# Top-k attention and a gated feed-forward: from pairs of heads to tiles of queries, with the mask on ScalarE and the gate on GpSimd

## The chip, the cores and the metric

The kernel runs on one core of one Trainium2 chip. The metric is the device time of one execution in microseconds (us). The engines are named as in the profile: PE is TensorE's matmuls and PEld its weight loads, DVE is VectorE, ACT is ScalarE, POOL is GpSimd, SP is SyncE, which here only issues DMAs.

## What is computed

Eight batches of eight heads attend over 576 tokens of 64 dimensions. Of every row of scores only the 32 largest (and what equals the 32nd) are kept. The result, 4608 tokens of 512, goes through two matrix products with a gate between them. The weights arrive in float64.

```python
def attention(q, k, v):                       # (8, 8, 576, 64) each, float32
    scores = np.matmul(q, k.transpose(0, 1, 3, 2)) / np.sqrt(64)
    kth = np.partition(scores, -32, axis=-1)[..., -32:-31]
    scores = np.where(scores >= kth, scores, -1e9)
    attn = np.exp(scores - scores.max(axis=-1, keepdims=True))
    attn = attn / (attn.sum(axis=-1, keepdims=True) + 1e-9)
    return np.matmul(attn, v)

def feed_forward(x, w_in, w_out):             # (4608, 512), (512, 2048), (2048, 512)
    h = x @ w_in
    return (h * np.cos(h)) @ w_out
```

## The kernel before

Attention goes by units: 128 queries of two heads (a pair), or the 64 left-over queries of both heads together in one tile. There are 160 units, 128 whole ones and 32 of 64 queries, so that DVE's work is that of 144 whole ones. They run batch by batch, and within a batch pair by pair; the five units of a pair follow one another.

`scores` (L111) lets PE write two tiles of 128 by 576 scores and ACT copy them to SBUF with the scale (L127). `softmax` finds the 32 largest on DVE: four rounds of MAX8 (L141), which gives the eight largest of a row, and three of MATCH_REPLACE (L153), which takes them out of a copy. After the first round POOL negates the maximum (L144) and ACT takes the exponential of all 576 (L146). After the fourth, DVE compares the scores with the 32nd, multiplies by the exponential and sums the row in one SCALAR_TENSOR_TENSOR (L156); then come the reciprocal on DVE (L167) and the normalising on POOL (L169). `transpose_p` (L191, L202) and `values` (L222) follow one unit behind, P times V only after two or three units, with 256 or 320 queries at once.

The feed-forward works on blocks of 384 tokens, three for every two batches. `ff1` (L250) makes two d_ff tiles of 384 tokens, ACT copies them out (L257), and POOL reduces the argument of the cosine in five instructions (L261 to L265). After every four items `gate` runs Abs (L270) and Sin (L272) on ACT and multiplies on DVE (L274). `ff2` (L280) needs a block's 16 tiles and makes 128 tokens by 512.

What sets the order is the loop at the end: scores one unit ahead, softmax, then as much of the feed-forward as a credit of streamed rows allows. A scheduler then gives each engine one fixed sequence, which the engine carries out in order. Weights are decoded from float64 in 16 pieces of 1024 columns, one per unit, by five DVE instructions, one of ACT and one of POOL each.

## Time and profile before

| | |
|---|---|
| three runs | 2244.55, 2256.88, 2257.63 us (median 2256.88) |
| profiled execution: span from first to last instruction | 2246.1 us (its own time is not listed apart) |
| PE / PEld / DVE / ACT / POOL busy | 1904.3 / 1020.7 / 1868.2 / 1059.5 / 985.9 us |
| mean granted TensorE clock | 0.887 of 2.4 GHz |
| DMA | 56.00 MB, mean 25 GB/s |

The profiled execution lies inside the spread of the runs, so its rows can be summed against the span; the median is 10.8 us above it. A float32 product of TensorE stands in the trace as two records, a transpose as one. Busy time counts overlapping instructions of an engine once, and a "mean ns of one" contains pipeline latency, so that rates are read from dense stretches.

### The profile page before, as it was taken

Reading aid. Unit: us, or ns where it says so; the run is one execution under the profiler, and the core shown is the slowest. Engines: PE = TensorE matmul, PEld = TensorE weight load, DVE = VectorE, ACT = ScalarE, POOL = GpSimd, SP = SyncE. Lnnn points to the kernel's source line nnn. Section 1 sums busy time; section 2 is a strip of 40 time slices with the busy share of each in tenths; the row PEclk is TensorE's granted clock in tenths of the full one; section 3 lists DMA queues with packets and bytes.
Section 4 is the critical chain, followed back from the end, with each engine's and each line's share of the span. In section 5 each row is a group of like instructions: output and inputs, shape, how many; then the busy total and the mean of one; then the engine's idle time right before and its main releaser. Section 6 shows DMA issues by size and latency. Waiting matters only on the chain.

```text
span 2246.1 us, 22954 instructions
## 1 busy us (share of the span) xinstructions
PE 1904.3 (85%) x7200; PEld 1020.7 (45%) x7200; DVE 1868.2 (83%) x3953; ACT 1059.5 (47%) x1706; POOL 985.9 (44%) x1078
## 2 busy tenths in 40 slices
PE   4556688978898898898899898898898898898878
PEld 2222244445644444446544444446544444447443
DVE  8999987998999979889998798998999799793000
ACT  3333355445545545645645635635645545643121
POOL 3444256114625524524725525615616515616362
PEclk9555688977999899899999899998898898999999
DMA  4222000000000000000000000000000000000000
GB/s 136 81 86 72 16 16 6 26 23 15 11 30 17 16 26 21 14 27 12 14 28 16 17 26 21 16 31 6 16 30 16 12 26 21 6 15 1 10 5 14
DMA packets 37305, 56.00 MB, mean 25 GB/s; under 512 B 2880, under 2 KB 21312, under 8 KB 36160
## 3 DMA queue, kind: packets, MB, share of 16 engines
q1 hardware_dynamic: 37184, 54.54, 7.4%
q8 instruction: 57, 0.93, 0.2%
q14 instruction: 64, 0.52, 0.1%
HBM read 45.09 MB, written 9.44 MB: 24 GB/s over the span
## 4 chain that ended last, share of the span: by engine, by line
DVE 36%; PE 22%; POOL 22%; ACT 10%; issue 10%; DMA 0%; POOLq 0%; SPq 0%; DVEq 0%; ACTq 0%
DVE m L141 14%; DVE rest L153 12%; PE o L280 8%; POOL r L264 6%; POOL r L265 5%; DVE pt L156 4%; PE sc L120 4%; POOL r L262 3%; POOL n L263 3%; PE o L222 3%; POOL n L261 3%; PE tp L191 2%; POOL pt L169 2%; ACT r L270 2%; ACT ht L257 2%
## 5 line engine op out<-in xcount | busy, mean ns | idle before, releaser
L141 DVE MAX8 m<-rest 128x8 f32<-128x576 f32 x864 | 616.2, 748 | 64.2 <-POOL neg L144 61.5
L280 PE MATMUL o<-w_out,ht 128*128 128x512 f32 x1152 | 539.3, 611 | 7.3 <-DVE ht L274 6.2
L120 PE MATMUL sc<-k,q 64*128 64x512 f32 (+3 forms) x1280 | 391.2, 518 | 164.9 <-ACT s L127 159.8
L153 DVE MATCH_REPLACE8 rest<-m,rest 128x576 f32<-128x576 f32 x576 | 423.7, 742 | 0.0
L120 PEld LDWEIGHTS sc<-k,q 64*128 64x128 f32 (+1 forms) x1280 | 165.7, 203 | 383.6 <-ACT s L127 215.9
L144 POOL TENSOR_SCALAR neg<-m 128x1 f32<-128x1 f32 x288 | 71.0, 251 | 599.0 <-DVE den L165 430.1
L169 POOL TENSOR_SCALAR pt<-pt,rden 128x576 f32<-128x576 f32 x288 | 253.2, 888 | 169.1 <-DVE rden L167 165.7
L280 PEld LDWEIGHTS o<-w_out,ht 128*128 128x128 f32 x1152 | 211.3, 194 | 233.0 <-issue 209.7
L156 DVE SCALAR_TENSOR_TENSOR pt<-s,m,pt 128x576 f32<-128x576 f32 x288 | 271.1, 974 | 53.0 <-ACT pt L146 52.7
L191 PE MATMUL tp<-ident,pt 128*128 128x128 f32 x1152 | 205.2, 322 | 116.8 <-POOL pt L169 114.6
L274 DVE TENSOR_TENSOR ht<-ht,r 128x768 f32<-128x768 f32 x96 | 100.1, 1054 | 214.2 <-ACT r L272 214.2
L146 ACT ACTIVATE pt<-s,neg 128x576 f32<-128x576 f32 x288 | 214.9, 772 | 113.0 <-POOL neg L144 112.1
L127 ACT ACTIVATE s<-sc 128x576 f32<-128x576 f32 (+1 forms) x320 | 201.5, 646 | 136.9 <-DVE pt L156 112.4
L191 PEld LDWEIGHTS tp<-ident,pt 128*128 128x128 f32 x1152 | 151.6, 162 | 230.7 <-POOL pt L169 195.6
L261 POOL TENSOR_SCALAR n<-ht 128x768 f32<-128x768 f32 x96 | 85.3, 888 | 378.5 <-ACT ht L257 375.2
L193 ACT COPY pT<-tp 128x512 f32<-128x512 f32 x256 | 141.3, 584 | 181.1 <-PE tp L191 179.0
L141 DVE MAX8 m<-s 128x8 f32<-128x576 f32 x288 | 214.2, 753 | 0.0
L153 DVE MATCH_REPLACE8 rest<-m,s 128x576 f32<-128x576 f32 x288 | 212.2, 742 | 0.0
L270 ACT ACTIVATE r<-r 128x768 f32<-128x768 f32 x96 | 81.0, 844 | 252.1 <-POOL r L265 252.1
L264 POOL TENSOR_TENSOR r<-r,ht 128x768 f32<-128x768 f32 x96 | 182.1, 1897 | 5.4
L265 POOL TENSOR_TENSOR r<-r,n 128x768 f32<-128x768 f32 x96 | 178.8, 1862 | 6.6
L222 PE MATMUL o<-pT,v 128*64 128x320 f32 (+1 forms) x1024 | 164.3, 471 | 0.9 <-ACT pT L196 0.5
(611 smaller groups left out, 2137.7 us busy)
## 6 DMA issues: line engine op xcount, KB each, us to landing
q<-in_q_dram SPq DMA_DIRECT2D x32, 288.0 KB, 2.9
k<-in_k_dram SPq DMA_DIRECT2D x32, 288.0 KB, 3.2
out_dram<-ob SPq DMA_DIRECT2D x36, 256.0 KB, 2.0
v<-in_v_dram SPq DMA_DIRECT2D x32, 256.0 KB, 2.8
st<-in_moe_w_in_dram SPq DMA_DIRECT2D x8, 1024.0 KB, 5.2
st<-in_moe_w_out_dram SPq DMA_DIRECT2D x8, 1024.0 KB, 4.9
v_tail<-in_v_dram SPq DMA_DIRECT2D x32, 32.0 KB, 2.4
```

The costliest lines, as they stand in the source:

```text
L120: nc.tensor.matmul(sc[j][rows[j], ks], st["q"][d, qs], st["k"][d, ks], start=True, stop=True)
L127: nc.scalar.mul(out=s[j % len(s)][rows[j]], in_=sc[j][rows[j]], mul=SCALE)
L141: nc.vector.max(m8[j], tops[j])
L146: nc.scalar.activation(out=pt[:, j], in_=s[j], func=AF.Exp, bias=neg[:, j : j + 1], scale=1.0)
L153: nc.vector.match_replace(rest[j], m8[j], tops[j], NEG)
L156: nc.vector.scalar_tensor_tensor(out=pt[:, j], in0=s[j], scalar=m8[j][:, 7:8], in1=pt[:, j], op0=ALU.is_ge, op1=ALU.mult, accum_out=den[:, ...
L169: nc.gpsimd.tensor_scalar(out=pt[:, j], in0=pt[:, j], scalar1=rden[:, j : j + 1], scalar2=1.0, op0=ALU.mult, op1=ALU.mult,)
L191: nc.tensor.transpose(tp[:, c], pt[:, j, c * P : (c + 1) * P], ident)
L222: nc.tensor.matmul(o[j * D : (j + 1) * D, 0:w], lhsT, rhs, start=c == 0, stop=c == NT)
L264: gp.tensor_tensor(out=r, in0=r, in1=ht, op=ALU.add)
L265: gp.tensor_tensor(out=r, in0=r, in1=n, op=ALU.add)
L280: nc.tensor.matmul(o[:, 0:DM], g[grp, blk, f // FI][:, f % FI, i * P : (i + 1) * P], w_out[:, f], start=f == 0, stop=f == NF - 1,)
```

## The change

The order of attention is now by tiles of queries: for one tile of 128 (or 64) queries all four pairs of heads follow one another, and P times V is done for each unit with its 128 (64) queries. Blocks of the feed-forward are 128 tokens (the first two and the last two) or 256 tokens, and are ready as soon as a tile, or two, of all heads are. The scores are taken two units ahead, in one PSUM tile with one copy of 1152 elements; `softmax`, transposes and P times V come one and two units later.

The mask leaves DVE. POOL makes two small numbers of the largest and the 32nd (`bounds`), ACT runs Prelu in place, whose slope for negative arguments is 2^100, and then Exp, which also sums the row. What is below the 32nd becomes so negative that its exponential is 0. DVE keeps MAX8, MATCH_REPLACE and the reciprocal.

In the feed-forward ACT already divides by 2 pi at the copy (L355), POOL reduces by four instructions of 1024 elements (L360 to L363), ACT runs Sin alone, and POOL multiplies (L379). The two products are cut into items: 512 columns of `ff1`, four d_ff tiles of `ff2`. `feed` picks one when its inputs are there, at two places of a unit. Weights are decoded in 32 pieces of 512 columns, four per unit, with three instructions each on ACT and DVE and two on POOL.

```diff
--- before.py
+++ after.py
...
-    BLK = 3 * P  # tokens in a block of the feed-forward
...
-    loads = ctx.enter_context(tc.tile_pool(name="loads", bufs=2))
+    loads = ctx.enter_context(tc.tile_pool(name="loads", bufs=5))
...
-    CW = 1024  # weights of a partition in a chunk
+    CW = 512
...
+        r = stage.tile([P, CW], I32, tag="lo", name="lo")
+        nc.scalar.mul(out=r, in_=lo.bitcast(U32), mul=2.0**-29)
+        sg = stage.tile([P, CW], F32, tag="sg", name="sg")
+        nc.scalar.sign(sg, hi)
+        nc.scalar.activation(out=w, in_=hi.bitcast(F32), func=AF.Abs)
+        nc.vector.tensor_scalar(out=w, in0=w, scalar1=2.0**-15, scalar2=None, op0=ALU.max)
+        nc.vector.tensor_scalar(
+            out=wi, in0=wi, scalar1=896 << 20, scalar2=3,
+            op0=ALU.bitwise_xor, op1=ALU.logical_shift_left,
+        )
+        nc.vector.tensor_scalar(
+            out=wi, in0=wi, scalar1=0x7FFFFFFF, scalar2=None, op0=ALU.bitwise_and
+        )
+        nc.gpsimd.tensor_tensor(out=wi, in0=wi, in1=r, op=ALU.add)
+        nc.gpsimd.tensor_tensor(out=w, in0=w, in1=sg, op=ALU.mult)
+    units = []
+    for b in range(B):
+        if b % 2 == 0:
+            tiles = [(i * P, P) for i in range(NT)] + [(MAIN, TAIL)]
+        else:
+            tiles = [(0, TAIL)] + [(TAIL + i * P, P) for i in range(NT)]
+        for q0, rows in tiles:
+            for hp in range(NP):
+                units.append({"b": b, "hp": hp, "q0": q0, "rows": rows, "tok": b * S + q0})
...
     def scores(u):
+        sc = ps.tile([P, 2, 2, 512], F32, tag="sc", name="sc", bufs=1)
+        for h in range(2):
+            for j in range(2):
+                d = slice(j * D, (j + 1) * D)
+                nc.tensor.matmul(
+                    sc[head_rows(u, j), j, h, 0:HS],
+                    st["q"][d, qs],
+                    st["k"][d, h * HS : (h + 1) * HS],
+                    start=True,
+                    stop=True,
+                )
+        s = work.tile([P, 2, S], F32, tag="s", name="s", bufs=5)
+        u["s"], u["n"] = s, u["rows"] * 2 // P
+        if u["n"] == 2:
+            nc.scalar.copy(
+                out=s.rearrange("p j (h w) -> p (j h) w", h=2),
+                in_=sc.rearrange("p j h w -> p (j h) w")[:, :, 0:HS],
+            )
+        else:
+            for j in range(2):
+                r = head_rows(u, j)
+                nc.scalar.copy(
+                    out=s[r, 0].rearrange("p (h w) -> p h w", h=2), in_=sc[r, j, :, 0:HS]
+                )
+    def topk_round(u, rnd):
+        s, n = u["s"], u["n"]
+        if rnd == 0:
+            u["m8"] = small.tile([P, 2, TOPK], F32, tag="m8", name="m8")
+            u["rest"] = work.tile([P, 2, S], F32, tag="rest", name="rest", bufs=1)
+        m8, rest = u["m8"], u["rest"]
+        src = s if rnd == 0 else rest
+        at = slice(8 * rnd, 8 * rnd + 8)
+        for j in range(n):
+            nc.vector.max(m8[:, j, at], src[:, j])
+        if rnd < TOPK // 8 - 1:
+            for j in range(n):
+                nc.vector.match_replace(rest[:, j], m8[:, j, at], src[:, j], NEG)
+        else:
+            del u["rest"]
+    def bounds(u):
+        n = u["n"]
+        nb = small.tile([P, 2, 2], F32, tag="nb", name="nb")
+        nc.gpsimd.tensor_scalar(
+            out=nb[:, 0:n], in0=u.pop("m8")[:, 0:n, 0 : TOPK : TOPK - 1], scalar1=-SCALE,
+            scalar2=1.0, op0=ALU.mult, op1=ALU.mult,
+        )
+        nd = small.tile([P, 2], F32, tag="nd", name="nd")
+        nc.gpsimd.tensor_tensor(
+            out=nd[:, 0:n], in0=nb[:, 0:n, 0], in1=nb[:, 0:n, 1], op=ALU.subtract
+        )
+        u["nb"], u["nd"] = nb, nd
+    def softmax(u):
+        s, n, nb, nd = u["s"], u["n"], u.pop("nb"), u.pop("nd")
+        for j in range(n):
+            nc.scalar.activation(
+                out=s[:, j], in_=s[:, j], func=AF.Prelu, bias=nb[:, j, 1:2], scale=SCALE, alpha=FAR
+            )
+        den = small.tile([P, 2], F32, tag="den", name="den")
+        for j in range(n):
+            nc.scalar.activation(
+                out=s[:, j], in_=s[:, j], func=AF.Exp, bias=nd[:, j : j + 1], scale=1.0,
+                accum_out=den[:, j : j + 1],
+            )
+        u["den"] = den
+    def reciprocal(u):
+        n, den = u["n"], u["den"]
+        nc.gpsimd.tensor_scalar(
+            out=den[:, 0:n], in0=den[:, 0:n], scalar1=1.0, scalar2=EPS, op0=ALU.mult, op1=ALU.add
+        )
+        rden = small.tile([P, 2], F32, tag="rden", name="rden")
+        nc.vector.reciprocal(rden[:, 0:n], den[:, 0:n])
+        u["rden"] = rden
+    def normalise(u):
+        s, rden = u["s"], u.pop("rden")
+        for j in range(u["n"]):
+            nc.gpsimd.tensor_scalar(
+                out=s[:, j], in0=s[:, j], scalar1=rden[:, j : j + 1], scalar2=1.0,
+                op0=ALU.mult, op1=ALU.mult,
+            )
...
-            nc.vector.scalar_tensor_tensor(
-                out=pt[:, j],
-                in0=s[j],
-                scalar=m8[j][:, 7:8],
-                in1=pt[:, j],
-                op0=ALU.is_ge,
-                op1=ALU.mult,
-                accum_out=den[:, j : j + 1],
-            )
...
+    widths = [P, P] + [2 * P] * (B * S // (2 * P) - 2) + [P, P]
...
+    CHUNKS = 5
+    ff = {"live": 0, "now": 0, "weights": 0}
+    first = deque((blk, i) for blk in blocks for i in range(NF * blk["w"] // 512))
+    second = deque(
+        (blk, i, f) for blk in blocks for i in range(blk["w"] // P) for f in range(0, NF, 4)
+    )
...
+    def ff1(blk, i):
...
+        nc.scalar.mul(out=g[:, half * 512 : half * 512 + 512], in_=mm, mul=INV_2PI)
+        if half == 0:
+            return
+        x = ffw.tile([P, 1024], F32, tag="x", name="x", bufs=3)
+        gp = nc.gpsimd
+        gp.tensor_scalar(out=x, in0=g, scalar1=1.0, scalar2=0.25, op0=ALU.mult, op1=ALU.add)
+        gp.tensor_scalar(out=x, in0=x, scalar1=1.0, scalar2=MAGIC, op0=ALU.mult, op1=ALU.add)
+        gp.tensor_scalar(out=x, in0=x, scalar1=-MAGIC, scalar2=1.0, op0=ALU.add, op1=ALU.mult)
+        gp.tensor_tensor(out=x, in0=g, in1=x, op=ALU.subtract)
+        waiting.append((blk, g, x, ff["now"]))
+    def sines(least):
+        ready = [c for c in waiting if c[3] < ff["now"]]
+        if not ready or (len(ready) < least and ready[0][3] + 4 > ff["now"]):
+            return
+        for blk, g, x, _ in ready:
+            waiting.popleft()
+            nc.scalar.activation(out=x, in_=x, func=AF.Sin, bias=halfpi, scale=TWO_PI_BELOW)
+            sined.append((blk, g, x))
+    def gates():
+        while sined:
+            blk, g, x = sined.popleft()
+            nc.gpsimd.tensor_tensor(out=g, in0=g, in1=x, op=ALU.mult)
+            blk["gated"] += 1
...
-        for r, ht in pending:
-            nc.vector.tensor_tensor(out=ht, in0=ht, in1=r, op=ALU.mult)
...
+    def feed():
+        if second:
+            blk, i, f = second[0]
+            if blk["gated"] * 1024 // blk["w"] >= f + 4 and ff["weights"] == len(chunks):
+                second.popleft()
+                ff2(blk, i, f)
+                return True
+        if first:
+            blk, i = first[0]
+            nf = 512 // blk["w"]
+            need = ((i + 1) * nf - 1) // FC * NC + NC
+            if blk["left"] == 0 and ff["weights"] >= need and (i % 2 or ff["live"] < CHUNKS):
+                first.popleft()
+                ff1(blk, i)
+                return True
+        return False
...
+        credit = min(credit + (u or x)["rows"] * 2.1 / P, 4.0)
+        ff["now"] += 1
+        if i + 2 < NU:
+            scores(units[i + 2])
+        if w:
+            bounds(w)
+        gates()
+        if u:
+            topk_round(u, 0)
+        decode(1)
+        if w:
+            softmax(w)
+        sines(2)
+        if credit >= 1 and feed():
+            credit -= 1
+        if u:
+            topk_round(u, 1)
+        decode(1)
+        if w:
+            reciprocal(w)
+            normalise(w)
+        if u:
+            topk_round(u, 2)
+        decode(1)
+        if x:
+            transpose_main(x)
+        while credit >= 1 and feed():
+            credit -= 1
+        if x:
+            transpose_tail(x)
+            values(x)
+        if u:
+            topk_round(u, 3)
+        decode(1)
+    while first or second:
+        ff["now"] += 1
+        gates()
+        sines(1)
+        if not feed():
+            ff["now"] += 4
```

How the order moves on DVE, in the middle of the program. Before, one unit (m_0 and m_1 are its two heads' eight largest, rest the copies):

```order
L141 MAX m_0_6165<-rest_6155 128x8
L141 MAX m_1_6166<-rest_6157 128x8
L153 MATCH_REPLACE rest_6155<-m_0_6165,rest_6155 128x576
L153 MATCH_REPLACE rest_6157<-m_1_6166,rest_6157 128x576
L141 MAX m_0_6171<-rest_6155 128x8
L141 MAX m_1_6172<-rest_6157 128x8
L156 SCALAR_TENSOR_TENSOR pt,den<-s_6044,m_0_6171,pt 128x576
L156 SCALAR_TENSOR_TENSOR pt,den<-s_6045,m_1_6172,pt 128x576
L141 MAX m_0_6242<-s_6140 128x8
L165 TENSOR_SCALAR den<-den 128x2
L141 MAX m_1_6243<-s_6141 128x8
L167 RECIPROCAL rden<-den 128x2
```

And now, one unit; the reciprocal belongs to the unit before it:

```order
L210 MAX m_5821<-s 128x8 x2
L213 MATCH_REPLACE rest<-m_5821,s 128x576 x2
L210 MAX m_5821<-rest 128x8 x2
L213 MATCH_REPLACE rest<-m_5821,rest 128x576 x2
L252 RECIPROCAL rden<-den 128x2
L210 MAX m_5821<-rest 128x8 x2
L213 MATCH_REPLACE rest<-m_5821,rest 128x576 x2
L210 MAX m_5821<-rest 128x8 x2
```

The two masking instructions are gone, and the reciprocal, which now needs ACT's sum of the unit before, stands two rounds into the next unit.

On POOL, before (n and r are the reduced argument, ht the block's h, pt the weights of attention):

```order
L169 TENSOR_SCALAR pt<-pt,rden 128x576
L261 TENSOR_SCALAR n<-ht 128x768
L262 TENSOR_SCALAR r<-n 128x768
L263 TENSOR_SCALAR n<-n 128x768
L264 TENSOR_TENSOR r<-r,ht 128x768
L265 TENSOR_TENSOR r<-r,n 128x768
L144 TENSOR_SCALAR neg<-m_0_8163 128x1
L144 TENSOR_SCALAR neg<-m_1_8164 128x1
```

And now, in a unit that carries a piece of 1024 elements (x and g are that piece, nb and nd the bounds of the unit, den its sum):

```order
L362 TENSOR_SCALAR x<-x 128x1024
L221 TENSOR_SCALAR nb<-m_7313 128x4
L363 TENSOR_TENSOR x<-g,x 128x1024
L226 TENSOR_TENSOR nd<-nb 128x2
L379 TENSOR_TENSOR g<-g,x 128x1024
L360 TENSOR_SCALAR x<-g 128x1024
L361 TENSOR_SCALAR x<-x 128x1024
L248 TENSOR_SCALAR den<-den 128x2
L221 TENSOR_SCALAR nb<-m_7410 128x4
```

Between a unit's nb and its den there are now a reduction, a gate and the first half of the next reduction.

On ACT, in the same unit (L235 is Prelu, L240 Exp, L373 Sin, L355 and L272 are copies out of PSUM for the feed-forward and the transposes):

```order
L373 ACT_TABLE_LOAD
L373 ACTIVATE x<-x,halfpi 128x1024
L235 ACTIVATE s<-s,nb 128x576
L355 ACTIVATE g<-mm 128x512
L272 COPY pT<-tp 128x4x128 x2
L235 ACTIVATE s<-s,nb 128x576
L240 ACT_TABLE_LOAD
L240 ACTIVATE s,den<-s,nd 128x576
L355 ACTIVATE g<-mm 128x512
L284 COPY pT_tail<-tp 64x256
L240 ACTIVATE s,den<-s,nd 128x576
```

The two Prelus and the two Exps of a unit are spread among a Sin, two table loads and five copies. Over the whole program there are 134 table loads.

## Rows read from the trace of the kernel before

**Rows 1.** The page, part 1: busy time, share, instructions of each engine.
```profile
PE 1904.3 (85%) x7200; PEld 1020.7 (45%) x7200; DVE 1868.2 (83%) x3953; ACT 1059.5 (47%) x1706; POOL 985.9 (44%) x1078
```

**Rows 2.** Windows: PE, PEld, DVE, ACT, POOL busy us; clock, DMA, GB/s.
```profile
1800.00:1900.00 100.00, 92.78 (x341) 46.79 (x340) 97.94 (x220) 47.01 (x79) 34.75 (x46) 0.94 0.09 26
...
2100.00:2200.00 100.00, 82.70 (x205) 41.60 (x206) 6.71 (x7) 20.49 (x34) 45.85 (x35) 0.93 0.02 8
```

**Rows 3.** Waits of DVE, 200 to 2060 us: total, times, longest.
```profile
DVE ht L274 <- ACT r L272: 73.6, 16, 11.2
DVE m L141 <- POOL neg L144: 61.5, 28, 6.8
DVE pt L156 <- ACT pt L146: 52.7, 20, 6.6
```

**Rows 4.** Timeline of DVE, one unit: start us, length us, instruction.
```profile
1819.68 0.75 DVE L141 MAX8 m<-s 128x8 f32<-128x576 f32 x1
...
1822.59 1.41 DVE L141 MAX8 m<-rest 128x8 f32<-128x576 f32 x2
...
1825.37 1.40 DVE L141 MAX8 m<-rest 128x8 f32<-128x576 f32 x2
...
1829.46 0.80 DVE L156 SCALAR_TENSOR_TENSOR pt<-s,m,pt 128x576 f32<-128x576 f32 x1
...
1830.93 0.75 DVE L141 MAX8 m<-s 128x8 f32<-128x576 f32 x1
```

**Rows 5.** Timeline of PE, five dense stretches.
```profile
1552.97 2.32 PE L222 MATMUL o<-pT,v 128*64 128x256 f32 x16
...
1822.66 1.04 PE L191 MATMUL tp<-ident,pt 128*128 128x128 f32 x8
...
1827.29 1.30 PE L120 MATMUL sc<-k,q 64*128 64x512 f32 x8
...
2151.10 2.74 PE L250 MATMUL hp__14007<-xT,w_in 128*128 128x384 f32 x8
...
2196.25 12.18 PE L280 MATMUL o<-w_out,ht 128*128 128x512 f32 x28
```

**Rows 6.** Groups by line and shape, ACT: busy us, mean ns | idle before.
```profile
L146 ACT ACTIVATE pt<-s,neg 128x576 f32<-128x576 f32 x288 | 214.9, 772 | 113.0 <-POOL neg L144 112.1
...
L127 ACT ACTIVATE s<-sc 128x576 f32<-128x576 f32 x256 | 160.3, 647 | 122.0 <-DVE pt L156 100.8 <-PE sc L120 18.0
...
L193 ACT COPY pT<-tp 128x512 f32<-128x512 f32 x256 | 141.3, 584 | 181.1 <-PE tp L191 179.0
...
L272 ACT ACT_TABLE_LOAD x59 | 75.7, 1283 | 1.0
```

**Rows 7.** The same view, POOL and DVE.
```profile
L264 POOL TENSOR_TENSOR r<-r,ht 128x768 f32<-128x768 f32 x96 | 182.1, 1897 | 5.4
...
L263 POOL TENSOR_SCALAR n<-n 128x768 f32<-128x768 f32 x96 | 90.6, 944 | 7.9
...
L274 DVE TENSOR_TENSOR ht<-ht,r 128x768 f32<-128x768 f32 x96 | 100.1, 1054 | 214.2 <-ACT r L272 214.2
...
L144 POOL TENSOR_SCALAR neg<-m 128x1 f32<-128x1 f32 x288 | 71.0, 251 | 599.0 <-DVE den L165 430.1 <-DVE m L141 80.4 <-ACT s L127 44.7
...
L344 DVE TENSOR_SCALAR x<-st 128x1024 int32<-128x1024 int32 x16 | 11.0, 690 | 8.8 <-DMA st<-in_moe_w_in_dram 8.8
```

**Rows 8.** Timeline of POOL: normalising, at the start and later.
```profile
26.34 3.95 POOL L169 TENSOR_SCALAR pt<-pt,rden 128x576 f32<-128x576 f32 x2 [9.20 <-DVE rden L167]
...
1821.43 1.47 POOL L169 TENSOR_SCALAR pt<-pt,rden 128x576 f32<-128x576 f32 x2
```

**Rows 9.** Timeline of DVE, end: last reciprocal, second and seventh gate after.
```profile
2041.01 0.17 DVE L167 RECIPROCAL rden<-den 128x2 f32<-128x2 f32 x1
...
2057.00 0.96 DVE L274 TENSOR_TENSOR ht<-ht,r 128x768 f32<-128x768 f32 x1 [7.31 <-ACT r L272]
...
2101.76 0.96 DVE L274 TENSOR_TENSOR ht<-ht,r 128x768 f32<-128x768 f32 x1 [7.29 <-ACT r L272]
```

431 lines of the change are left out of this document (172 added, 259 removed).

## The prediction

> **What bounds the kernel now.** The page's first part comes first: PE is busy 85% of the span, DVE 83%, ACT and POOL under half [rows 1]. Neither of the two is full, so the question is which waits hold both back, and the windows come next: in a middle stretch PE is busy 92.8 of 100 us at a granted clock of 0.94 and DVE 97.9; after 2100 us DVE does 6.7 us in 100 [rows 2]. So there are a middle, in which DVE is close to its limit, and an end without it.
>
> The middle by units: DVE's timeline shows a whole unit without waits taking 1830.93 - 1819.68 = 11.25 us, of which the two masking instructions take 1830.93 - 1829.46 = 1.47, and one round of MAX8 and MATCH_REPLACE for both heads 1825.37 - 1822.59 = 2.78 [rows 4]. Gates add 96 x 1.05 / 144 = 0.7 us [rows 7], so DVE needs about 11.95. The last reciprocal of attention ends at 2041 us [rows 9]; (2041 - 12 of start) / 144 = 14.1 us is what a unit takes. The 2.1 us between are the decoding of the weights (by 16 x 5 x 0.690 / 144, about 0.4 [rows 7]) and waits: for ACT's Sin before a gate 73.6 us, for POOL's small negation 61.5, for the exponential 52.7 [rows 3].
>
> PE by dense stretches [rows 5]: a unit's eight score records (512 and 64 columns, 2304 in all) 1.30 us; a transpose 1.04 / 8 = 0.13; a record of P times V with 256 columns 2.32 / 16 = 0.145; of ff1 with 384 columns 2.74 / 8 = 0.343; of ff2 12.18 / 28 = 0.435. Per unit: 1.30 + 10 x 0.13 + 1280 x 0.145 / 144 + 1536 x 0.343 / 144 + 1152 x 0.435 / 144 = 11.0 us. So PE has room, its 92.8 being partly slow clock and latency.
>
> The end: 2246.1 - 2041.0 = 205 us in which only the last feed-forward is left, and its gates come every (2101.76 - 2057.00) / 5 = 8.95 us [rows 9], a pace that POOL's chain, ACT and the copies set, not PE.
>
> **The change, part by part.** The sum goes by whole units (128), half units (32), the start and the end.
>
> DVE, whole unit: the mask (1.47) and the small addition (about 0.1) go, the gate goes, and nothing comes but a reciprocal that was there before: 11.25 - 1.57 = 9.7 us, half that for a half unit.
>
> PE, whole unit: scores have the same columns, 1.30; transposes the same, 1.30. P times V now has 20 records of 128 columns: 2.9 us if a record of 128 costs what one of 256 does, 1.45 if half; I take 1.8, nearer the half, since the larger records of rows 5 go by their columns (0.343 for 384, 0.435 for 512). An item of ff1 is 16 records of 256 columns, 16 x 0.343 x 256 / 384 = 3.66; one of ff2 eight records, 3.48; the blocks need one of each per unit, 7.14. Sum 11.5 us (11.2 to 12.6): more than DVE, because of the narrower P times V. A half unit: 1.30 + 0.65 + 1.0 + 3.6 = 6.5.
>
> ACT, whole unit: the copy of 1152 at most 2 x 0.647, Prelu and Exp 1.49 each (214.9 / 288 for one), two copies for the transposes 2 x 141.3 / 256 = 1.10 [rows 6]; smaller copies about 0.6, the copy for the gate 0.58, half a Sin of 1024 (by the row of 576) 0.7, a quarter of an output copy and two halves of a table load (1.283) 1.4: 8.7 us. Abs is gone. Prelu has no row; I price it as Exp. If it cost no more than a copy (0.58), 0.3 a unit would come off; if twice as much, 1.5 would come on. The sum in Exp may cost a small instruction more; the nearest row is POOL's small one, 0.251 [rows 7].
>
> POOL, whole unit: normalising 1.47 [rows 8], three small ones at 0.25, and half a piece: three single-input instructions at 0.944 x 1024 / 768 = 1.26, two of two inputs at 1.897 x 1024 / 768 = 2.53 [rows 7], 8.8 in all, 4.4 per unit: 6.6 us. The start shows normalising at 3.95 us where the later unit shows 1.47 [rows 8], while DVE decodes; after the start DVE has only instructions beside which POOL ran at 1.47.
>
> So no engine is over 11.5 and the coupling decides. DVE's reciprocal now waits, two rounds (5.56 us) into the next unit, for nb, nd, two Prelu, two Exp and den: 0.25 + 0.25 + 1.49 + 1.49 + 0.25 and five hand-overs (0.3 by estimate) = 4.0 us. In units that carry no piece it is there in time. Where a piece is carried, the order rows put a Sin, a table load, two copies for the gate, three for the transposes and, on POOL, a reduction's last step, a gate and two first steps ahead of den. Adding these in their order gives about 10.5 us, so the unit takes 10.5 + 4.2 (the rounds behind the reciprocal) = 14.7. Of eight units that feed a block of 256 tokens, four carry a piece; read in the order, two have the whole of it (14.7 and 15.2), one only ACT's part (12.2), one POOL's (10.7), and four take 9.7: 91.6 / 8 = 11.45 us. That is PE's 11.5, and two chains of equal length that wait for each other lose something: I take **12.0** for a whole unit (11.2 if PE alone counts at its low end, 13.4 if as much is lost as now, 2.1 on top of 11.3) and 7.0 for a half one (6.5 to 8).
>
> The start: scores need a copy of q and k, as now, about 10 us. Eight units then decode four pieces each: DVE 9.7 + 12 x 0.35 (0.690 for 1024 columns) = 13.9, POOL 8 x 1.26 + 2.3 or, by 3.95, 4.7 = 12.4 to 14.8 [rows 7, 8], ACT 7.2 + 5.9 = 13.1: 15 us, 8 x 15 + 10 = 130 (122 to 160 if transfers come late; now a unit there takes about 15 too).
>
> The end: after the last P times V the order has 96 products of ff1 with 128 columns (192 x 0.114 = 22 us) and 40 of ff2 (80 x 0.435 = 35), 57 on PE; the last two pieces pass POOL's 6.3 + 2.5, partly bare, about 15; the last unit's way from DVE to PE takes 12. Together 85 us (75 to 95) in place of 205.
>
> **Sum:** 130 + (128 - 8) x 12.0 + 32 x 7.0 + 85 = 1879 us of span, against 2246.1. The runs lie between 1.6 below and 11.5 above that span, so I add 5: **1885 us**.
>
> A page against the change: on POOL the two-input instruction takes 1.897 us, on DVE 1.054 for the same 768 elements [rows 7]. The Trainium skill, "GPSIMD Engine Reference", section "Engine selection", says just that, to do elementwise work on VectorE since GpSimd is about twice as slow with two inputs; the rows agree with the factor. By that rule alone the gate should have stayed; by the rows it leaves an engine at 9.7 + 0.7 for one at 6.6, and the rule becomes the third rival.
>
> A second page: one table load takes 1.283 us, with 1.0 us of idle before all 59 [rows 6]. The Trainium skill, "ScalarE: Activation LUTs", section "What ACT_TABLE_LOAD costs", counts 2.66 us with a drain for a switch; the row doesn't show the drain. By that figure, an estimate, ACT would need 1.3 us more per unit, and the sum would be about 100 us higher.
>
> **The rivals.** *PE alone counts.* Scores are taken two units ahead and five score buffers let DVE run ahead, so the long and the short units of DVE even out. For it: PE's order has an item beside every copy that it waits for. Against it: two consecutive long units are 7 us over. 122 + 120 x 11.2 + 32 x 6.5 + 75 + 5 = 1755 us.
>
> *The waits stay as long as they are now.* For it: the three waits of rows 3 turn into one chain through POOL, ACT and POOL again. 130 + 120 x 13.4 + 32 x 8.0 + 85 + 5 = 2084 us.
>
> *Slower: POOL's queue holds back den.* POOL works in order, and reduction, gate and next reduction (8.8 us) stand between nb and den. If a gate waits for a Sin that itself waits behind Prelu on ACT, all is added up: 4.0 + 6.4 on ACT + 8.8 + 4.2 = 23.4 us in each of the four units with a piece, 9.7 in the others, mean 16.5: 130 + 120 x 16.5 + 32 x 8.5 + 90 + 5 = 2477. From a mean of (2257 - 5 - 130 - 224 - 85) / 120 = 15.1 us on, the kernel is slower than before. Against it: in the order Sin stands before Prelu, and pieces come in half the units.
>
> **How the numbers follow.** The forecast (1800 to 1960 us) gets 0.50: DVE loses 2.2 us a unit for certain and the end 120. PE alone 0.23, the waits of now 0.17 (and up to 2120), the slower one 0.06, anything else that eats the gain 0.04. The range takes in the first rival and most of the second: 1745 to 2060. Faster by over 1% (about what a measurement of this kernel can tell from no change) 0.91, within 1% 0.03, slower 0.06.
>
> **What would show it.** DVE's busy time falls to about 1600 us; MAX8 to MAX8 of the next unit takes 9.7 us where no piece is carried and 14 to 15 where one is, with the idle time before the reciprocal, released by POOL's den; POOL's instructions of 1024 at 1.26 and 2.5 us; a record of P times V with 128 columns at 0.07 to 0.11 us; from the last reciprocal to the end 85 us. It is wrong if DVE never waits before the reciprocal (then 1755 or less), if PE's P times V costs 0.145 a record (a unit of 12.6 on PE), or if the first eight units take over 160 us.

## The result

The changed kernel takes 1914.61 us (median of 4 runs, 1908.91 to 1921.21) against 2254.4 us (4 runs, 2244.55 to 2257.63) for the kernel before in the same comparison: a ratio of 0.851, 95% interval 0.848 to 0.854. The forecast was 1885 us in a range of 1745 to 2060. The profiled execution after has a span of 1907.1 us, 28 us above the forecast's sum of 1879. One of the four executions of the kernel with three edits, further below, ran at a granted clock of 0.655 throughout and took 2417 us; its ratio leaves it out.

By stages the 339 us between the two spans lie thus (starts of units are the first MAX8 of a unit; the last reciprocal closes attention):

| stage | before | after | difference |
|---|---|---|---|
| start of the program to start of unit 16 | 246.1 | 234.1 | -12.0 |
| from there to the last reciprocal | 1794.9 | 1553.8 | -241.1 |
| last reciprocal to the end | 205.1 | 119.2 | -85.9 |

### The profile after

Part 1 of the page, which answers to [rows 1]:

```profile
PE 1708.2 (90%) x9632; PEld 1112.8 (58%) x9632; DVE 1483.7 (78%) x3137; ACT 1232.1 (65%) x2146; POOL 953.1 (50%) x1198
```

DVE has lost 384.5 us of work, more than the span did; PE is now the fullest engine. Its mean granted clock is 0.969 where it was 0.887; that is a rival for a part of the gain, and what it alone is worth no run here separates. Windows, with the columns of [rows 2], for the start, a middle stretch and the end:

```profile
0.00:100.00 100.00, 52.34 (x228) 32.66 (x229) 90.21 (x187) 73.02 (x126) 69.09 (x73) 1.00 0.55 174
100.00:200.00 100.00, 75.37 (x491) 53.63 (x491) 88.91 (x181) 66.92 (x116) 74.73 (x75) 0.85 0.14 46
...
1200.00:1300.00 100.00, 95.08 (x533) 62.41 (x534) 88.73 (x192) 70.71 (x123) 52.46 (x68) 0.98 0.04 12
...
1788.00:1907.00 119.00, 92.62 (x484) 59.60 (x482) 0.10 (x1) 19.86 (x33) 40.63 (x27) 0.92 0.03 10
```

In the middle PE is at 95 and DVE at 89, the reverse of [rows 2]. In the first 100 us DVE is busy for 90 us and PE for about half of them. The waits that DVE and PE name, over the whole span (total us, times, longest):

```profile
DVE m L210 <- ACT s L190: 136.4, 58, 8.9
DVE rden L252 <- POOL den L248: 132.4, 64, 9.3
DVE m L210 <- ACT s L197: 28.2, 19, 3.7
```

```profile
PE o L303 <- ACT pT_tail L284: 54.4, 41, 5.0
PE o L391 <- POOL g L379: 35.8, 7, 14.8
PE tp L283 <- ACT pT L272: 18.9, 20, 1.8
```

DVE waits 297 us in these three rows: for the copy of the scores, which follows PE's score records, and for den. Read by itself, the second row says that POOL's den holds DVE back. The experiments ask whether that is a cause or only the place where DVE waits for a slower engine.

A unit that carries a whole piece, from DVE's timeline (start us, length, instruction, idle time before it and what ended it), only its first and last rounds, the reciprocal and the start of the next unit:

```profile
1445.15 1.40 DVE L210 MAX8 m<-s 128x8 f32<-128x576 f32 x2
...
1453.46 1.41 DVE L210 MAX8 m<-rest 128x8 f32<-128x576 f32 x2
1457.75 0.17 DVE L252 RECIPROCAL rden<-den 128x2 f32<-128x2 f32 x1 [2.88 <-POOL den L248]
1459.85 1.42 DVE L210 MAX8 m<-s 128x8 f32<-128x576 f32 x2 [1.93 <-ACT s L190]
```

This unit takes 1459.85 - 1445.15 = 14.7 us, one of the two figures forecast for a unit that carries a whole piece, but not by the forecast's sum. The forecast had den at 10.5 us and two rounds (4.2 us) behind it. Here all four rounds are done first (9.7 us); then come 2.88 us of waiting for den, which arrives 12.6 us into the unit, and 1.93 us for the scores, a wait that the forecast did not have. The eight units of a cycle late in the program take 10.4, 9.7, 14.8, 11.9, 9.7, 14.7, 11.5 and 14.3 us: 97.0, or 12.1 a unit. Three of the eight are over 14 us where the forecast's order had two, and two are at 9.7 where it had four.

One unit of PE from a stretch without waits, which answers to [rows 5]:

```profile
1238.22 1.24 PE L180 MATMUL sc<-k,q 64*128 64x288 f32 x8
1239.39 3.72 PE L348 MATMUL mm<-xT,w_in 128*128 128x256 f32 x16
1242.95 1.04 PE L270 MATMUL tp<-ident,s 128*128 128x128 f32 x8
1243.82 3.62 PE L348 MATMUL mm<-xT,w_in 128*128 128x256 f32 x16
1247.28 0.38 PE L283 MATMUL tp<-ident,s 128*64 128x128 f32 x2
1247.59 1.09 PE L303 MATMUL o<-pT,v 128*64 128x128 f32 x16
1248.61 0.44 PE L303 MATMUL o<-pT_tail,v_tail 64*64 64x128 f32 x4
1248.98 1.24 PE L180 MATMUL sc<-k,q 64*128 64x288 f32 x8
```

From scores to scores PE takes 1248.98 - 1238.22 = 10.76 us, where the forecast had 11.5 (this unit carries two items of `ff1`, not one of each product, which is within 0.1 us by the forecast's prices); P times V takes (1248.98 - 1247.59) = 1.39 in place of the assumed 1.8, at 1.02 / 16 = 0.064 us a record.

Groups of ACT and POOL by line and shape (busy us, mean ns | idle before), for the prices of [rows 6 to 8]:

```profile
L235 ACT ACTIVATE s<-s,nb 128x576 f32<-128x576 f32 x288 | 215.4, 772 | 153.5 <-POOL nb L221 153.1
...
L373 ACT ACT_TABLE_LOAD x67 | 86.0, 1283 | 1.2
L240 ACT ACT_TABLE_LOAD x66 | 84.7, 1283 | 1.3
...
L240 ACT ACTIVATION_READ_ACCUMULATOR s<-s,nd 128x1 f32 x288 | 54.7, 190 | 0.0
```

```profile
L379 POOL TENSOR_TENSOR g<-g,x 128x1024 f32<-128x1024 f32 x72 | 170.1, 2362 | 63.3 <-ACT x L373 62.8
...
L363 POOL TENSOR_TENSOR x<-g,x 128x1024 f32<-128x1024 f32 x72 | 170.5, 2368 | 1.7
```

### The profile page after: what moved, and what is told of

Read it like the earlier page. It is cut to its first block, busy times and chain, and to the rows that moved or that the text cites. A ratio compares the mean times of both kernels' runs of the same rounds, so it can differ in the third digit from the quotient of the medians.

```text
span 1907.1 us, 26842 instructions
## 1 busy us (share of the span) xinstructions
PE 1708.2 (90%) x9632; PEld 1112.8 (58%) x9632; DVE 1483.7 (78%) x3137; ACT 1232.1 (65%) x2146; POOL 953.1 (50%) x1198
## 4 chain that ended last, share of the span: by engine, by line
DVE 26%; PE 25%; POOL 25%; ACT 19%; issue 4%; DMA 0%; POOLq 0%; SPq 0%; ACTq 0%
DVE m L210 13%; DVE rest L213 11%; PE o L391 10%; POOL x L363 7%; PE mm L348 7%; ACT s L240 4%; POOL x L361 3%; POOL s L258 3%; POOL x L362 3%; POOL x L360 3%; PE o L303 3%; ACT s L235 3%; PE sc L180 3%; ACT x L373 3%; POOL g L379 2%
## 5 line engine op out<-in xcount | busy, mean ns | idle before, releaser
L348 PE MATMUL mm<-xT,w_in 128*128 128x256 f32 (+1 forms) x2560 | 551.7, 371 | 27.4 <-ACT g L355 13.9
L391 PE MATMUL o<-w_out,g 128*128 128x512 f32 x1152 | 539.9, 612 | 35.8 <-POOL g L379 35.8
L348 PEld LDWEIGHTS mm<-xT,w_in 128*128 128x128 f32 x2560 | 452.0, 197 | 118.9 <-issue 29.0
L391 PEld LDWEIGHTS o<-w_out,g 128*128 128x128 f32 x1152 | 212.4, 194 | 276.8 <-issue 233.7
L210 DVE MAX8 m<-s 128x8 f32<-128x576 f32 x288 | 205.5, 748 | 164.6 <-ACT s L190 136.4
L235 ACT ACTIVATE s<-s,nb 128x576 f32<-128x576 f32 x288 | 215.4, 772 | 153.5 <-POOL nb L221 153.1
L180 PE MATMUL sc<-k,q 64*128 64x288 f32 (+1 forms) x1280 | 270.4, 461 | 21.9 <-ACT s L190 14.1
L258 POOL TENSOR_SCALAR s<-s,rden 128x576 f32<-128x576 f32 x288 | 215.8, 757 | 132.9 <-DVE rden L252 108.1
L240 ACT ACTIVATE s<-s,nd 128x576 f32<-128x576 f32 x288 | 221.8, 771 | 18.3 <-POOL nd L226 16.3
L379 POOL TENSOR_TENSOR g<-g,x 128x1024 f32<-128x1024 f32 x72 | 170.1, 2362 | 63.3 <-ACT x L373 62.8
L270 PE MATMUL tp<-ident,s 128*128 128x128 f32 x1152 | 161.1, 280 | 16.6 <-POOL s L258 12.6
L363 POOL TENSOR_TENSOR x<-g,x 128x1024 f32<-128x1024 f32 x72 | 170.5, 2368 | 1.7
L272 ACT COPY pT<-tp 128x512 f32<-128x512 f32 x256 | 137.5, 584 | 26.0 <-PE tp L270 25.6
```

The lines of the kernel that those rows point to most:

```text
L180: nc.tensor.matmul(sc[head_rows(u, j), j, h, 0:HS], st["q"][d, qs], st["k"][d, h * HS : (h + 1) * HS], start=True, stop=True,)
L210: nc.vector.max(m8[:, j, at], src[:, j])
L235: nc.scalar.activation(out=s[:, j], in_=s[:, j], func=AF.Prelu, bias=nb[:, j, 1:2], scale=SCALE, alpha=FAR)
L240: nc.scalar.activation(out=s[:, j], in_=s[:, j], func=AF.Exp, bias=nd[:, j : j + 1], scale=1.0, accum_out=den[:, j : j + 1],)
L258: nc.gpsimd.tensor_scalar(out=s[:, j], in0=s[:, j], scalar1=rden[:, j : j + 1], scalar2=1.0, op0=ALU.mult, op1=ALU.mult,)
L270: nc.tensor.transpose(tp[:, c], s[:, j, c * P : (c + 1) * P], ident)
```

## The experiments

Two theories of the steady part: **A**, PE's work sets the pace and the other engines wait for it wherever their order has them wait; **B**, the chain over POOL, ACT, POOL and DVE to the reciprocal sets it. Start, end and the single parts of the change have runs of their own. The order on each engine is set when the program is built by a scheduler with its own durations, so an edit also moves some instructions around it; differences of under 10 us are not read as the edit's alone. Times are medians of 4 runs (6 for one, 3 for another), ratios are to the kernel before on the same chip; the changed kernel's is 0.851 (0.848 to 0.854). Chips differ: the kernel before has medians of 2248 to 2254 us on them, so the ratios decide what can be told apart. A whole unit takes 11.46 us in the changed kernel's profile and 11.51 in those of the two runs that edit only the end or the second product's start, so 0.05 us of a unit is no effect.

### Less work for PE

```
-        for f in range(f0, f0 + 4):
+        for f in range(f0, f0 + 2):
...
-                o, g[:, at : at + P], w_out[f], start=f == 0, stop=f == NF - 1
+                o, g[:, at : at + P], w_out[f], start=f == 0, stop=f == NF - 3
```

> Half of the second product's records (the matmuls on every third and fourth of four d_ff tiles) are left out, so what comes out is half of the feed-forward's sum; nothing else changes. PE has about 4 x 0.435 = 1.74 us less per whole unit and about 35/2 us less in the end. Theory A (PE's work sets the pace of the steady part): a whole unit falls from 11.46 to about 10 us, units where nothing is carried stay at DVE's 9.7, the time falls by 150 to 200 us, to about 1740. Theory B (the chain nb, Prelu, Exp, den, reciprocal over POOL, ACT and DVE sets it): a whole unit stays over 11 us, the idle time before the reciprocal stays near 132 us or grows, and the time falls by 20 to 50 us, most of it in the end.

1700.01 us, ratio 0.757 (0.755 to 0.758), 215 us less. The 576 records left out are worth 576 x 0.435 = 251 us by [rows 5], so the program became shorter by 86% of what was taken off PE. A whole unit falls from 11.46 to 10.41 us, a half one from 8.13 to 6.55. The waits of DVE:

```profile
DVE rden L252 <- POOL den L248: 104.7, 76, 8.5
DVE m L210 <- ACT s L190: 13.2, 2, 10.1
```

```profile
400.00:500.00 100.00, 92.14 (x552) 61.22 (x554) 95.95 (x207) 77.97 (x134) 57.41 (x74) 0.98 0.14 44
```

The wait for the copied scores is nearly gone (136.4 to 13.2) although nobody touched ACT's copy: it had been PE all along. In the window DVE is at 96 us in 100 and PE at 92, so neither has much room left. The long units go too: 22 of the 119 whole units after the start took over 14 us in the changed kernel, here one does. This is the unit that took 14.7 us above:

```profile
1313.30 1.39 DVE L210 MAX8 m<-s 128x8 f32<-128x576 f32 x2
...
1321.75 0.17 DVE L252 RECIPROCAL rden<-den 128x2 f32<-128x2 f32 x1 [1.51 <-POOL den L248]
...
1324.60 1.41 DVE L210 MAX8 m<-s 128x8 f32<-128x576 f32 x2
```

It takes 11.3 us with the same work on ACT, POOL and DVE, and den is there 8.4 us into the unit instead of 12.6. Theory A, and more than it expected; what stays of B is den's 104.7 us, about 0.7 a unit.

### More room for den

```
         decode(1)
-        if w:
-            reciprocal(w)
-            normalise(w)
         if u:
             topk_round(u, 2)
...
             topk_round(u, 3)
         decode(1)
+        if w:
+            reciprocal(w)
+            normalise(w)
```

> Reciprocal and normalising are issued after the last top-k round of the next unit instead of after its second, so DVE has 4.2 us more before it needs den. Theory A (PE sets the pace): the 132 us of idle time before the reciprocal go, idle time turns up elsewhere, and the time stays within 15 us of 1915. Theory B (the wait for den sets the pace): the wait falls below 40 us and the time falls by 60 to 110 us. A third way: the transposes of that unit come 4.2 us later on PE, the wait of PE for the transposed copies grows, and the time rises by up to 60 us.

1913.55 us, ratio 0.851 (0.850 to 0.852): no change.

```profile
DVE rden L252 <- POOL den L248: 128.7, 65, 10.5
DVE m L210 <- ACT s L190: 124.8, 60, 8.9
```

Neither the time nor the wait moved, though DVE needs den 4.2 us later. So den's wait is no shortfall of some fixed chain that more room would cover; den comes as late as the units before it let it. Theory A had the time right, and the prediction, made with both theories, that this wait would go was wrong.

### Other work between PE's copies

```
-        if credit >= 1 and feed():
-            credit -= 1
         if u:
             topk_round(u, 1)
...
             transpose_main(x)
-        while credit >= 1 and feed():
+        if credit >= 1 and feed():
             credit -= 1
         if x:
             transpose_tail(x)
+        while credit >= 1 and feed():
+            credit -= 1
+        if x:
             values(x)
```

> The feed-forward's first item of a unit is moved on PE from before the transposes to behind those of the main part, and the second from before the tail's transposes to behind them, so that each of ACT's three copies for the transposes has an item of 3.5 us of PE's beside it. Amount of work: the same. If PE sets the pace and its waits for copies (pT_tail 54 us, pT 19 us) cost time, they fall below 20 us together and the time falls by 30 to 60 us. If another wait takes their place (PE for POOL's normalised s, or ACT's queue later), the time stays within 10 us. Where the chain of den sets the pace, nothing changes either, but the waits of PE grow at another place.

1917.69 us, ratio 0.852 (0.850 to 0.854): no change, and the waits of PE show why:

```profile
PE tp L270 <- ACT xT L308: 35.9, 31, 3.2
PE tp L283 <- ACT pT L272: 32.3, 29, 3.0
PE mm L348 <- ACT g L355: 24.8, 14, 3.9
PE o L303 <- ACT pT_tail L284: 24.0, 20, 5.1
```

pT_tail fell from 54.4 to 24.0 us; a new wait for xT (35.9) and longer ones for pT (18.9 to 32.3) and g (13.9 to 24.8) took its place. All of these are waits for copies of ACT: another record behind a copy moved the wait and did not shorten it.

### The gate back on DVE

```
-            nc.gpsimd.tensor_tensor(out=g, in0=g, in1=x, op=ALU.mult)
+            nc.vector.tensor_tensor(out=g, in0=g, in1=x, op=ALU.mult)
```

> The gate product goes back from POOL to DVE; all else stays. POOL has 72 x 2.37 = 170 us less, DVE 72 x about 1.4 = 101 us more, about 0.65 us per whole unit. Theory A (PE's work sets the pace): DVE's units of 9.7 become up to 10.4 on average, still under PE's 11.5, so the time stays within 15 us of 1915, and DVE's idle time shrinks by about what it took on. Theory B (the chain over POOL sets it): the chain loses up to 2.4 us in half of the units, and the time falls by 30 us or more. If the gate waits for a Sin on DVE and holds back the rounds behind it, the time rises by 30 us or more.

1932.83 us, ratio 0.859 (0.857 to 0.860), 18 us slower: between the first and the third case. POOL's busy time falls by 151.7 us and DVE's wait for den from 132.4 to 74.8, but DVE has a new wait, here from 200 to 1800 us:

```profile
DVE m L210 <- ACT s L190: 87.9, 41, 4.0
DVE rden L252 <- POOL den L248: 64.2, 43, 6.3
DVE g L379 <- ACT x L373: 47.3, 34, 5.0
```

A gate that waits for its Sin holds the rounds behind it, 47.3 us; a whole unit takes 11.65 in place of 11.46 to 11.51. So the move of the gate brought about 1% of the time. The rows put it down to a wait taken out of DVE's queue, not to speed: the instruction itself takes 1.23 us on DVE (median) and 2.36 on POOL. The forecast's third rival, POOL's queue in den's way, is there in these rows (132.4 against 74.8 us of waiting), but it is the cheaper of the two waits.

### The mask back on DVE

```
-                out=s[:, j], in_=s[:, j], func=AF.Prelu, bias=nb[:, j, 1:2], scale=SCALE, alpha=FAR
+                out=e, in_=s[:, j], func=AF.Exp, bias=nb[:, j, 0:1], scale=SCALE
...
-            nc.scalar.activation(
-                out=s[:, j], in_=s[:, j], func=AF.Exp, bias=nd[:, j : j + 1], scale=1.0,
+            nc.vector.scalar_tensor_tensor(
+                out=s[:, j], in0=s[:, j], scalar=u["m8k"][:, j, TOPK - 1 : TOPK], in1=u["e"][j],
+                op0=ALU.is_ge, op1=ALU.mult, accum_out=den[:, j : j + 1],
```

> The mask goes back from ACT's Prelu to one DVE instruction per head that also sums the row (1.47 us per whole unit), the small addition goes back to DVE; ACT has 288 x 0.772 = 222 us and 288 x 0.190 = 55 us less, and POOL's den goes. A DVE unit without waits is 9.7 + 1.6 = 11.3 us, as long as PE's 11.5. Theory A (PE's work sets the pace, and DVE lay below it): the time rises by 20 to 80 us, since two engines of equal length wait for each other. Theory B (ACT and POOL's chain sets the pace): the time falls. If DVE were the bound of the changed kernel, the time would rise by 144 x 1.6 = 230 us.

1980.63 us, ratio 0.880 (0.878 to 0.882), 66 us slower, in A's range. Besides the lines shown, the run writes the exponentials to tiles of their own and has one output buffer of the feed-forward instead of two. A middle window:

```profile
1300.00:1400.00 100.00, 93.33 (x476) 59.67 (x475) 100.00 (x217) 51.77 (x76) 47.48 (x54) 0.93 0.09 30
```

DVE is now full and PE close to it. The mask on ACT is worth these 66 us and not the 144 x 1.6 = 230 us of DVE that it frees, since a whole unit takes 12.1 us with the mask on DVE and 11.46 with it on ACT: what DVE gained beyond that, PE did not follow.

### The order of the units back to pairs of heads

```
-        for q0, rows in tiles:
-            for hp in range(NP):
+        for hp in range(NP):
+            for q0, rows in tiles:
```

> Only the order of the units goes back: all queries of a pair of heads, then the next pair, in place of all pairs for a tile of queries. A batch's feed-forward can then start only with the last pair of the batch, and that of the last batch is left for the end: of its 576 tokens about 450 come after the last pair has begun, some 3.5 whole blocks of 128 at 7.1 us x 4 of PE, 100 us, less what is left over now (119 us, of which about 90 of PE's records). The time rises by 60 to 140 us. If it rises by less than 20, the order of the units is not what took the old end of 205 us away.

1984.31 us, ratio 0.881 (0.879 to 0.883), 70 us slower. Unlike what was put down for it, the run changes more than the order: to make room for six xT buffers instead of three it has fewer buffers for q, k and v (one less each) and one output buffer instead of two. The last reciprocal comes earlier (1734.5 against 1787.9 us), the end is 247.0 us in place of 119.2; PE is busy 194 of 250 us there:

```profile
1730.00:1980.00 250.00, 194.15 (x773) 120.45 (x771) 0.17 (x1) 38.85 (x58) 90.10 (x59) 0.92 0.02 8
```

Over the whole run PE waits 4.5 us for a load (7.8 in the changed kernel), and nothing waits for the output buffer, so the buffers don't show in these times: the order of the units is what shortened the end. It pays for it with 53 us in attention, since the feed-forward's work then lies there. Of the end's 128 us, some 70 are won.

### The start without GpSimd's part of decoding

```
-        nc.gpsimd.tensor_tensor(out=wi, in0=wi, in1=r, op=ALU.add)
-        nc.gpsimd.tensor_tensor(out=w, in0=w, in1=sg, op=ALU.mult)
```

> The two GpSimd instructions of a weight piece (adding the low bits, multiplying by the sign) are left out, so the weights are not those of the reference. Theory C (DVE's decoding instructions are slow in the start because GpSimd's two-input instructions run beside them): the masking and shifting instruction falls from 0.8 to about 0.4 us on DVE, a unit of the start from 17.1 to about 15, the first whole unit after it starts 15 to 20 us earlier, and the time falls by 10 to 20 us. Theory D (the price is DVE's own, or ACT sets the pace of the start): the instruction stays at 0.8 us, or the unit at 16 to 17 us.

1897.25 us, ratio 0.843 (0.841 to 0.845), 17 us faster. The first eight units take 15.2 us each in place of 17.1. DVE's decoding rows from 0 to 150 us (busy us, mean ns | idle before), of the changed kernel and of this one:

```profile
L120 DVE TENSOR_SCALAR w_in<-w_in 128x512 int32<-128x512 int32 x16 | 12.6, 789 | 0.0
...
L124 DVE TENSOR_SCALAR w_in<-w_in 128x512 int32<-128x512 int32 x16 | 8.6, 540 | 0.0
```

```profile
L120 DVE TENSOR_SCALAR w_in<-w_in 128x512 int32<-128x512 int32 x16 | 6.8, 425 | 0.0
L124 DVE TENSOR_SCALAR w_in<-w_in 128x512 int32<-128x512 int32 x16 | 6.7, 416 | 0.0
```

Theory C. Alone the instruction takes 0.42 us; beside POOL's two-input instructions it nearly doubles. The pieces of the second product's weights, which now meet POOL's work on the feed-forward, still stand at 0.62 us.

### Two weight pieces per unit

```
         if u:
             topk_round(u, 0)
-        decode(1)
...
             topk_round(u, 2)
-        decode(1)
```

> Two weight pieces are decoded per unit instead of four, over sixteen units instead of eight. If the first eight units take 17.1 us each because decoding adds its DVE instructions at a fixed price, the first sixteen units take as long as now (137 + 8 x 9.7 = 215 us), and the time changes by at most 10 us for that part; the feed-forward starts its second product 80 us later and the backlog of PE's work grows, so the time rises by 20 to 60 us if PE sets the pace, and by less than 15 if it does not. If the price comes from POOL's decoding beside DVE's, the decoding instruction on DVE falls from 0.82 toward 0.40 us and the first sixteen units take about 195 us.

1902.4 us, ratio 0.847 (0.845 to 0.848), 12 us faster (10 by the ratios) where 20 to 60 slower was expected of A. The shifting instruction (L120) falls to 0.465 us (10 to 90 us), but the first sixteen units take 219.1 us against 224.7 in the changed kernel, not the 195 expected with it: that part missed. PE gets more to do early, not less: its first product starts at 39 us instead of 58, and it is busy 65.09 and 75.68 us in the first two windows against 52.34 and 75.37 above. Most of the gain comes behind the start: unit 16 starts 4 us earlier, the last unit 17 us earlier. That it is these 13 us of PE's work, done early, fits A and was not tested apart. The feared backlog at the end is small (125.6 us from the last reciprocal to the end).

### The end on DVE, and the second product earlier

```
+        ff["end"] = i > NU
...
-        gp = nc.gpsimd
+        gp = nc.vector if ff["end"] else nc.gpsimd
...
-            nc.gpsimd.tensor_tensor(out=g, in0=g, in1=x, op=ALU.mult)
+            (nc.vector if ff["end"] else nc.gpsimd).tensor_tensor(out=g, in0=g, in1=x, op=ALU.mult)
```

> After the last unit the range reduction and the gate are DVE's, which is idle there, instead of POOL's. If the end is 119 us instead of 85 because PE waits for POOL's gates (2.6 + 6.5 + 10.1 us), those waits shrink and the time falls by 10 to 20 us. If the end is long because PE lags DVE and its own records fill it, the time falls by less than 5 us.

1908.62 us, ratio 0.849 (0.848 to 0.850): 6 us less, between the two cases, but the intervals of the ratios overlap, so the time alone doesn't tell it from no change. The profiles do, for the end: PE still waits 9.6 us for gates where the changed kernel waits 19.3, and the end takes 109.9 us in place of 119.2. The larger part of the end is PE's own records.

```
-            if blk["gated"] * 1024 // blk["w"] >= f + 4 and ff["weights"] == len(chunks):
+            if blk["gated"] * 1024 // blk["w"] >= f + 4 and ff["weights"] >= len(chunks) - NF + f + 4:
```

> The second product may begin once the four pieces of weights that it reads are decoded, instead of all 32; nothing else changes. If PE sets the pace and its idle time in the start (127 of the first 200 us are busy) is lost for good, work that moves into it is won: PE does up to 16 items (56 us) of the second product earlier, of which the gates let perhaps a third be in time, so the time falls by 5 to 25 us. If the five buffers of gate pieces or the gates themselves hold it back, nothing changes (within 4 us).

1913.57 us, ratio 0.848 (0.846 to 0.850), against the changed kernel's 0.851: no difference that can be told. PE is busy 125.5 of the first 200 us, as before, and the second product starts at 138.8 us, 2.4 behind the first gate, as in the changed kernel (137.9, 2.4 behind it); the decoded weights were not what it waited for.

### Three edits together

> Three changes together: two weight pieces per unit, the second product begun early, range reduction and gate on DVE after the last unit. If PE's idle time is what each took away, the gains add up: 12 + 10 + 6, about 1887 us. If the first two take the same idle time away, about 1897.

1892.17 us (median of three), ratio 0.840 (0.838 to 0.842): 22 us, 1.2%, better than the changed kernel, between the two sums. It joins the second product early and the end on DVE with two pieces per unit, but leaves out the `decode` calls behind the second and the fourth round, where the run above left out those behind the first and the third; so it is not the sum of the three runs. The last run adds to it:

```
-        credit = min(credit + (u or x)["rows"] * 2.1 / P, 4.0)
+        credit = min(credit + (u or x)["rows"] * (3.0 if i < 32 else 2.1) / P, 4.0)
```

> As the one before it, and in the first 32 units up to three feed-forward items are taken per whole unit instead of 2.1. If PE's idle time in the first 300 us is still there because items are held back by the rate, the time falls by 10 to 20 us more; if they are held back by what is ready (blocks, gates, buffers), it stays within 4 us, and if longer units in the start make DVE wait, it rises by up to 10.

1900.37 us, ratio 0.843 (0.841 to 0.846): the higher rate brings nothing. The intervals overlap, so it lies between "stays" and "rises by up to 10"; whether what is ready holds the items back in the start, or longer units there cost what the rate gains, is not shown.

## Why the prediction was right, and where its terms were off

The frame held: DVE's work fell under PE's, the units kept a part of their waits, and the end shrank with the order of the units. Of its cases it was the forecast's own, not a rival's. Inside that frame the forecast's account of a long unit, a chain over POOL and ACT to den of 10.5 us, did not hold, and part of the closeness is luck: the sum was 28 us too low, of four terms that missed by more than that and partly cancelled:

| term | forecast | measured | difference |
|---|---|---|---|
| start to unit 8 | 130 | 146.4 | +16.4 |
| 119 whole units | 1428 (12.0) | 1363.3 (11.46) | -64.7 |
| 32 half units | 224 (7.0) | 260.3 (8.13) | +36.3 |
| last unit and end | 97 (12 + 85) | 137.1 | +40.1 |

**The start, 130.** The step that failed here is the 0.35 us for a decoding instruction of 512 columns on DVE, half of the row for 1024 [rows 7]. The row came from a stretch in which POOL normalised beside the decoding and did its two-input instruction later, beside MAX8 and MATCH_REPLACE. After the change POOL's two-input work lies beside the decoding, as DVE's and POOL's timelines show together:

```profile
70.25 0.83 DVE L120 TENSOR_SCALAR w_in<-w_in 128x512 int32<-128x512 int32 x1
71.00 0.75 DVE L210 MAX8 m<-rest 128x8 f32<-128x576 f32 x1
71.67 0.40 DVE L124 TENSOR_SCALAR w_in<-w_in 128x512 int32<-128x512 int32 x1
...
73.00 0.97 DVE L120 TENSOR_SCALAR w_in<-w_in 128x512 int32<-128x512 int32 x1
```

```profile
69.45 1.34 POOL L128 TENSOR_TENSOR w_in<-w_in,sg 128x512 f32<-128x512 f32 x1
...
72.42 1.26 POOL L127 TENSOR_TENSOR w_in<-w_in,lo 128x512 int32<-128x512 int32 x1
```

The instruction at 70.25 began inside POOL's (69.45 to 70.79) and took 0.83 us; the one at 71.67 stood between two of POOL's and took 0.40; the one at 73.00 began inside the next (to 73.68) and took 0.97: both ended 0.29 us after POOL's did. MAX8 is 0.75 throughout. The Trainium skill, "SBUF — State Buffer", section "SBUF: two separate sides", says that a port pair shared by VectorE and GpSimd is an exclusive lock, held for a whole instruction, which a VectorE instruction takes if it runs in a two-port mode or, against a GpSimd instruction that reads SBUF, has two SBUF inputs. The rows agree as far as they go: the TENSOR_SCALAR that starts second ends just behind POOL's instruction, and MAX8 does not wait; in which mode it runs no row shows. Without POOL's part the first eight units take 15.2 us each, which is the forecast's 15, and unit 8 starts at 131.0 us.

**A whole unit, 12.0.** The late cycle takes 12.1, and its long units 14.7, both as forecast, but the second by luck: the step that failed is den's fixed 10.5 us with two rounds behind it. With PE's work cut, the same unit takes 11.3 us and all but one of the units over 14 are gone; with 4.2 us more room for den, 19 of the 119 are still over 14, where the changed kernel has 22. So the length of a long unit came from PE, not from that chain. The mean over all 119 is 11.46, because the units after the start take 9.7 while PE's feed-forward has not yet caught up. PE's own 11.5 was 0.7 too high (P times V 0.4, the scores, transposes and items 0.3). That the coupling of two nearly equal chains costs something was right; the forecast had left open which of the two sets the pace, and the run with less work for PE answers it: PE. The rival by which PE alone counts had the right engine and left out the loss: to PE's 10.76 us a mean unit adds 0.7, one of the late cycle 1.3.

**Prelu and the rest of ACT and POOL.** Prelu at Exp's price was right to the nanosecond (772). The reading of the sum was bounded by 0.251 us and takes 0.190. POOL came out below the forecast: 1.05 and 2.36 us in place of 1.26 and 2.53. The table loads, now 133, have 2.5 us of idle time before all of them together. The figure of the Trainium skill, "ScalarE: Activation LUTs", section "What ACT_TABLE_LOAD costs", with its drain of another 1.38 us, is not what these rows show either.

**A half unit, 7.0.** The second group of eight half units takes 15.6, 11.2, 6.2, 9.0, 6.4, 6.6, 8.1 and 6.2 us. The first two are as long as whole units, the others lie around the 7.0; without the first two the mean is 7.1. The term counted each unit's work where DVE starts it, but PE is then still at the whole units before. That this lag is the cause is read from PE's order, not tested; with less work for PE the mean half unit falls to 6.55 us.

**The end, 85.** In the main the same lag. The forecast left 96 products of ff1 and 40 of ff2 for the time after the last P times V (192 and 80 records); counted from the last reciprocal, the trace has 263 and 108, and PE is busy 92.6 of the 119 us, against 57 and the 12 of the last unit's way. The last P times V ends 32 us after the last reciprocal, not 12; from there the records are the forecast's 192 and 80, and they take 87 us in place of 72. PE is busy 61 of these, so the bare part is 26 us where 15 were assumed. Most of it is in these rows:

```profile
1852.25 7.13 PE L391 MATMUL o<-w_out,g 128*128 128x512 f32 x16 [2.63 <-POOL g L379]
...
1871.05 8.97 PE L391 MATMUL o<-w_out,g 128*128 128x512 f32 x16 [6.53 <-POOL g L379]
...
1893.68 9.59 PE L391 MATMUL o<-w_out,g 128*128 128x512 f32 x16 [10.10 <-POOL g L379]
```

They hold 19.3 us in three waits, of which the run with the end on DVE took half away; the rest is short waits for ACT's copies and 4 us behind PE's last record.

**What would have shown it wrong.** DVE's busy time was to fall to about 1600 us and fell to 1483.7; the 1600 was mis-sized, since the forecast's own terms, 144 x 9.7 us and 96 x 0.35 for the decoding, come to 1430; the row for V was to lie between 0.07 and 0.11 us and is 0.064; the first eight units were to stay under 160 us and did.

What stays open is the 0.7 us a unit (1.3 in the late cycle) that PE's dense 10.76 doesn't explain. The clock can be a part of it, and is untested: the dense unit ran at a granted clock of 1.00, the windows of the middle at 0.95 to 1.00. Moving the reciprocal and moving the feed-forward's items only moved the waits. Nothing that shortens ACT's queue alone, at the same work on PE and DVE, was tried.

## What to carry to other kernels

A wait's name is the place where an engine stands, not the reason: DVE's largest waits were for ACT's copy and POOL's den, giving den 4.2 us more room changed nothing, and taking records off PE took the first one away. Where two engines come out close to each other, as PE and DVE here, leave out work of one and read the time before any order is rearranged. When work is priced by a row, look at what ran beside that row, and count a lagging engine's work at the place where that engine does it: the lag here came back in the end, where the last P times V was 32 us behind the last reciprocal instead of 12. And a figure that comes out as forecast, like the 14.7 us here, shows its cause only when its parts do.

## What the runs showed of the hardware

- A TENSOR_SCALAR of 512 elements on DVE (L120) took 0.41 to 0.42 us with nothing on POOL when it began. Of its 32 runs 26 began inside a two-input instruction of POOL; all of these took 0.75 to 1.90 us and ended 0.28 to 0.29 us behind it. MAX8 of 576 stayed at 0.73 to 0.76 in both cases.
- Records of P times V, which write one or the other half of the partitions by turns, cost 1.02 / 16 = 0.064 us for 128 columns in a dense stretch at a granted clock of 1.00; those of ff1 over all partitions with 128 columns stand at 3.84 / 32 = 0.12 us in the end, at 0.92. The first cost about half; why, no run here asked.
- Here an ACTIVATE with a sum brings a second instruction, the read of the accumulator, of 0.190 us: 54.7 us for 288 of them.
